# The tail of an attention and mixture kernel takes its PSUM banks in the order of their simulated release

## The chip, the cores and the metric

The kernel runs on one core of a Trainium2 chip. The metric is the device time of one execution in microseconds (us); what counts is the median of several executions. A profiled execution has its own time, and its span (first to last instruction) lies inside that time.

## What is computed

Sliding-window attention with sinks over 4 batches of 8 heads, 768 positions and 64 dimensions, and behind it a soft mixture of 8 experts over the 3072 tokens that come out. The part that this change touches is the mixture's end:

```python
slot_input = (d.T @ x).reshape(E, S_per_e, D)          # 8 experts, 4 slots each, D = 512
for e in range(E):
    h = np.maximum(slot_input[e] @ w1[e], 0.0)         # first layer, F = 1024
    slot_out[e] = h @ w2[e]                            # second layer
return (c @ slot_out.reshape(n_slots, D)).astype(np.float32)   # combine: 3072 x 512
```

All of it is float32. The two weight tensors hold 32 MB, the output 6.29 MB.

## The kernel before

The program has two parts that stand one behind the other on every engine.

The first part is the attention and everything up to `slot_input` (called `si` in the code) and the combine weights. Its steps are written down as entries of a `Plan`, and `Plan.order` simulates them with written-out costs: for each engine a list in `ORDER` fixes which step follows which, and the simulation only interleaves the engines and hands out the eight PSUM banks (512 floats per partition each). `Plan.issue` then emits the instructions. A step that opens a PSUM tile takes a bank that the simulation holds free; the step that reads the tile last gives it back. `banks[b]` is the simulated time at which bank b came free.

The last steps of this part are: `finish` (fin.0 to fin.10), which builds `si` and the factors `rz`; the softmax over slots of the last batch (sm.0 to sm.4); and `turn` (tr.0 to tr.26), nine times two transposes on TensorE with a copy out of PSUM into `ct`, the transposed combine weights. The program's names show `ct` and its sources as `pts` or `qt`, since they lie in those buffers. In VectorE's list of `ORDER` the end reads `..., 922, 926, 966, 927, 929, 963, 930, 969, 925`. In words: the copy of `si` out of PSUM, the softmax's row minimum, a `turn` copy, two softmax steps, a `turn` copy, a softmax step, a `turn` copy, and the reciprocal that ends `finish`.

The second part is `Moe.tail`, emitted in the order in which it is written. It takes its PSUM tiles through `InOrder`, a plan whose `add` runs each step at once. `InOrder` has a fixed rotation: the pair of banks 0 and 1 for the one wide tile (`op`, line 564), and banks 2, 3, 4, 5, 6, 7, 2, ... in turn for all others (`at`, lines 284 to 292). The tail does:

- `first(0, k)` for k = 0 to 3 into two new banks `hp`: 32 matmuls of 512 columns, `si` against weight tiles `wts[0]` to `wts[7]`. Four matmuls on four column groups of the array stand side by side. Each float32 matmul is two rows of the trace.
- `relu(0)`, then `first(1, k)` into two new banks, with `turned(0)` (eight transposes, two banks) behind k = 1, then `relu(1)` and three more `turn` steps.
- `second(r, k, h)`: 96 matmul groups of 256 columns against `wts[16]` to `wts[31]`, into the wide pair `op`.
- `split(h)` and `combine(n, h)`: 24 combine tiles, each copied out of PSUM and sent to the output, 16 transfers of 256 KB and 4 of 512 KB on SyncE's queue.

The weights lie in 21 slots that are used in rotation. Twenty-three weight tiles are loaded by the first part. The last nine are asked for inside the tail by `more(n)`: two behind `first(0, 0)`, two behind `first(0, 1)`, one behind `relu(0)`, and four in the second round. Each goes into a slot that TensorE has to have read first, so these loads wait for the tail's matmuls. All loads and all outputs stand in SyncE's one queue.

Of the kernel before, what the change touches and what calls it, by code (L numbers as in the profile page):

```python
# [125 lines left out]
class Engine:  # L126


    def __init__(self, tc, engine):
        self.tc, self.engine = tc, engine  # L130
# [19 lines left out]
class Plan:  # L150
# [17 lines left out]
    def add(self, key, eng, time, fn, r=(), w=(), new=None, last=None, mode=(128, 128), size=0):  # L168

        self.steps.append((key, eng, time if isinstance(time, tuple) else (time,) * len(eng), fn, tuple(r), tuple(w),  # L170
                           self.some(new), self.some(last), mode if isinstance(mode[0], tuple) else (mode, mode), size))
# [22 lines left out]
    def order(self):  # L194
        steps, self.opened = self.steps, set()
        before = self.depends()
        nxt, left, ready = [[] for _ in steps], [len(d) for d in before], [0.0] * len(steps)
        for i, d in enumerate(before):
            for x in d:
                nxt[x].append(i)  # L200
        closers = {}
        for st in steps:
            for h in st[7]:
                closers[h["name"]] = closers.get(h["name"], 0) + 1
        ends, free, banks = dict.fromkeys(closers, 0.0), dict(self.START), dict.fromkeys(range(8), 0.0)
        todo = {e: list(reversed(o)) for e, o in ORDER.items()}
        on = {i: e for e, o in ORDER.items() for i in o}
        order, mode, place, since = [], (128, 128), 0, 0.0
        while len(order) < len(steps):
            best = None  # L210
            for e, o in todo.items():
                if not o or left[o[-1]]:
                    continue
                i = o[-1]
                t, new = max(free[e], ready[i]), steps[i][6]
                if new:
                    if new[0]["kind"] == "s":
                        x = min((max(banks[y], banks[y + 1]) for y in range(0, 8, 2) if y in banks and y + 1 in banks), default=None)
                    else:
                        x = sorted(banks.values())[len(new) - 1] if len(banks) >= len(new) else None  # L220
                    if x is None:
                        continue
                    t = max(t, x)
                if best is None or t < best[0]:
                    best = (t, e)
            at, e = best
            i, t0 = todo[e].pop(), at
            _, eng, times, _, _, _, new, last, modes, size = steps[i]
            time = times[eng.index(e)]
            if e == "P":  # L230
                t0 += self.SWITCH * (modes[0] != mode)
                mode = modes[1]
            for h in new:
                if h["kind"] == "s":
                    b = max((x for x in range(0, 8, 2) if x in banks and x + 1 in banks
                             and max(banks[x], banks[x + 1]) <= at + 1e-9), key=lambda x: (max(banks[x], banks[x + 1]), -x))
                    h["bank"] = (b, b + 1)
                else:
                    b = max((x for x in banks if banks[x] <= at + 1e-9), key=lambda x: (x ^ 1 not in banks, banks[x], -x))
                    h["bank"] = (b,)  # L240
                for x in h["bank"]:
                    del banks[x]
            end = t0 + time
            place += size
            if place >= self.BLOCK:
                place -= self.BLOCK
                t = end - (end - t0) * place / size
                end += max(0.0, since + self.FETCH - t)
                since = max(t, since + self.FETCH)
            free[e] = end  # L250
            for h in last:
                x = h["name"]
                ends[x], closers[x] = max(ends[x], end + self.LAT), closers[x] - 1
                if closers[x] == 0:
                    for b in h["bank"]:
                        banks[b] = ends[x]
            for x in nxt[i]:
                ready[x] = max(ready[x], end + (0.05 if on[x] == e else self.DMA_LAT if e == "D" else self.LAT))
                left[x] -= 1
            order.append((t0, len(order), i, e))  # L260
        return order

    def issue(self):
# [17 lines left out]

class InOrder(Plan):

    at = 2


    def add(self, key, eng, time, fn, r=(), w=(), new=None, last=None, mode=None, size=0):
        for h in self.some(new):
            if h["kind"] == "s":
                h["tile"] = self.place("s", 0)  # L290
            else:
                h["tile"], self.at = self.place("w", self.at), 2 + (self.at - 1) % 6
        fn(eng[0])

    def tile(self, kind="w"):
# [5 lines left out]
class Moe:  # L301
# [207 lines left out]
        plan.add(keys[0], "P", 0.44, go, r=[("cs", x, y)], w=[h["name"]], new=h)  # L509
        plan.add(keys[1], *(("AV", (0.27, 0.33)) if u % 2 else ("VA", (0.33, 0.27))), out, r=[h["name"]], w=[("ct", b, u)], last=h)  # L510

    def tail(self, slot, wts, more, out):
        nc, c, B, si, pool = self.nc, self.c, self.B, self.si, InOrder(self.pools)
        hp, hs, ht = [], None, None

        def first(r, k):
# [50 lines left out]
        def second(r, k, h):  # L567
            for j in range(4):
                if r == 0 or k < 4:
                    w, o = wts[16 + 8 * r + 4 * (k // 4) + j], 512 * (k % 4) + 256 * h  # L570
                else:
                    w, o = wts[28 + 2 * h + k % 4 // 2], 1024 * (k % 2) + 256 * j
                nc.tensor.matmul(op[32 * j:32 * j + 32, h, 0:256], lhsT=ht[:, k, r, j].rearrange("p q i -> p (q i)"),
                                 rhs=w[:, o:o + 256], start=(r == 0 and k == 0), stop=(r == 1 and k == 7),
                                 skip_group_check=True)

        def split(h):
            hi, x = tw[:, 0, 256 * h:256 * h + 256], op[:, h, 0:256]
            nc.scalar.copy(hi, x)
            nc.vector.scalar_tensor_tensor(tw[:, 1, 256 * h:256 * h + 256], hi.bitcast(F32), c.lo_rows, x,  # L580
                                           op0=ALU.mult, op1=ALU.add)
# [4 lines left out]
        def combine(n, h):  # L586
            if h == 0 and n % 2 == 0:
                obs.append(slot().rearrange("p (n i m) -> p n i m", n=2, i=2))
            cols, yp, ob = slice(256 * h, 256 * h + 256), pool.tile(), obs[n // 2][:, n % 2]
            for i in range(2):  # L590
                nc.tensor.matmul(yp[:, 256 * i:256 * i + 256], lhsT=self.ct[n // 3][:, n % 3, i, :], rhs=tw[:, 1, cols],
                                 start=(i == 0), stop=(i == 1), skip_group_check=True)
            (nc.vector.tensor_copy if (n + h) % 2 else nc.scalar.copy)(
                ob[:, :, cols], yp.rearrange("p (i m) -> p i m", i=2))
            if n < HALF:
                nc.sync.dma_start(ov[:, n, :, cols], ob[:, :, cols])
            elif h:
                nc.sync.dma_start(ov[:, n], ob)
# [12 lines left out]
        for k in range(4):  # L611
            second(1, k, 1)
        for n in range(HALF - 2):
            combine(n, 0)
        for k in range(4, 8):
            second(1, k, 1)
        split(1)
        for n in range(HALF - 2, HALF):
            combine(n, 0)
        for n in range(HALF):  # L620
            combine(n, 1)
        for n in range(HALF, 12):
            combine(n, 0)
# [27 lines left out]


NSLOT = 24
HALF = 8
WARM = 8, 10, 24
PT = 4
KIND = {'kt': 'w', 'q': 'w', 'T': 'w', 'sk': 'w', 'xn': 'w', 'x': 'w'}
ORDER = {"P": [
# [63 lines left out]
def window_path(ctx, tc, c, moe, q, k, v, phi, w1, w2, out):  # L722
# [12 lines left out]
    fr = ctx.enter_context(tc.tile_pool(name="fr", bufs=1))  # L735
    slots = ctx.enter_context(tc.tile_pool(name="slots", bufs=NSLOT - 3))

# [286 lines left out]

    for x in range(WARM[1]):
        h = plan.psum()
        add((f"warm.{x}", 0, 0.0), "P", 0.42, lambda e, h=h: busy(e, h), new=h, last=h)

    for n, (b, j) in enumerate(jobs):
        def t(name, k=None, off=0.0, n=n):  # L1030
            return (name, n, off) if k is None else [(f"{name}.{x}", n, off) for x in range(k)]
# [22 lines left out]
        if j == NJ - 1:  # L1054
# [3 lines left out]
            moe.slot_softmax(plan, t("sm", 5), b, [("lg", b, x) for x in range(NJ)] + last)  # L1058
    for i in range(NSLOT - 7):
        add((f"w.{i}", 0, 0.0), "D", 2.6, lambda e: weight())  # L1060
# [20 lines left out]
def window_rest(tc, moe, plan, weight, weights, wts, slot, out):  # L1081
    plan.issue()

    def more(n):
        for _ in range(n):
            weight()

    weights.load(moe.first[1][:, 0:2048])
    moe.nc = Core(tc, ("tensor",))
    moe.tail(slot, wts, more, out)  # L1090


def general_path(ctx, tc, c, moe, ints, q, k, v, phi, w1, w2, out):
# [126 lines left out]
def fused(ctx, tc, q, k, v, n_sink, window, phi, w1, w2, out):  # L1220
# [24 lines left out]
    t = pools[:, 7]  # L1245
    for _ in range(WARM[0]):
        nc.tensor.matmul(t[:, 0:P], lhsT=c.ident, rhs=c.ident, start=True, stop=True)  # L1247
# [47 lines left out]
```

## Time and profile before

| | |
|---|---|
| three executions | 231.56 us median, 228.77 to 233.5 |
| the profiled execution: time | 226.95 us |
| its span | 225.1 us |
| TensorE busy | 196.9 us (87%), mean granted clock 0.955 |
| VectorE, ScalarE, GpSimd busy | 154.9 us, 149.9 us, 131.2 us |
| transfers | 59.50 MB, mean 264 GB/s |
| first part of the program on TensorE | 0 to 168.7 us |
| tail on TensorE | 171.0 to 210.1 us |

All rows are of the one profiled execution; times run from its span's start. In the views of single instructions PE is TensorE's matmul, PEld its weight load, DVE VectorE, ACT ScalarE and SP SyncE, and a group that touches the work of others gives in square brackets how long the engine stood idle before it and which instruction ended that. Most instructions of both parts carry line 136, a recording helper; they are told apart by tile names. The busy time of PE is modelled, so its end is rough.

### The profile page before, as it was taken

Reading aid. Unit: us, or ns where it says so; the run is one execution under the profiler, and the core shown is the slowest. Engines: PE = TensorE matmul, PEld = TensorE weight load, DVE = VectorE, ACT = ScalarE, POOL = GpSimd, SP = SyncE. Lnnn points to the kernel's source line nnn. Section 1 sums busy time; section 2 is a strip of 40 time slices with the busy share of each in tenths; the row PEclk is TensorE's granted clock in tenths of the full one; section 3 lists DMA queues with packets and bytes.
Section 4 is the critical chain, followed back from the end, with each engine's and each line's share of the span. In section 5 each row is a group of like instructions: output and inputs, shape, how many; then the busy total and the mean of one; then the engine's idle time right before and its main releaser. Section 6 shows DMA issues by size and latency. Waiting matters only on the chain.

```text
span 225.1 us, 9484 instructions
## 1 busy us (share of the span) xinstructions
PE 196.9 (87%) x3730; PEld 138.3 (61%) x3730; DVE 154.9 (69%) x423; ACT 149.9 (67%) x614; POOL 131.2 (58%) x274
## 2 busy tenths in 40 slices
PE   7899897999999999999979999998996999999400
PEld 7766675777676767667867766766651235667300
DVE  4499994698989888988967799897784013007600
ACT  2399888699999989989977989987241113016500
POOL 2248988686879988977777699899440320000000
PEclk9999998899999999999978999999996999999955
DMA  4856989983999799899898999799994899977994
GB/s 113 191 133 138 284 202 256 336 194 75 217 284 300 192 267 323 237 222 292 262 315 191 276 215 338 226 416 335 342 416 167 298 425 379 348 237 240 336 359 197
DMA packets 91623, 59.50 MB, mean 264 GB/s; under 512 B 77236, under 2 KB 85428, under 8 KB 90036
## 3 DMA queue, kind: packets, MB, share of 16 engines
q1 hardware_dynamic: 91572, 58.83, 86.7%
q8 instruction: 31, 0.51, 0.9%
q14 instruction: 20, 0.16, 0.2%
HBM read 52.53 MB, written 6.29 MB: 261 GB/s over the span
## 4 chain that ended last, share of the span: by engine, by line
PE 63%; DVE 10%; ACT 8%; POOL 4%; issue 4%; DMA 3%; SPq 1%; ACTq 0%; DVEq 0%; POOLq 0%
PE ps L136 61%; ACT pts L136 6%; DVE first L136 2%; DVE small L136 2%; DMA wt<-in_v_dram 2%; DVE ps L136 2%; PE ps L1247 2%; POOL pts L136 1%; DMA first<-in_k_dram 1%; POOL small L136 1%; ACT first L136 1%; POOL wt L136 1%; SPq L136 1%; DVE wt L136 1%; ACT qt L136 1%
## 5 line engine op out<-in xcount | busy, mean ns | idle before, releaser
L136 ACT ACTIVATE pts<-ps,small 128x132 f32<-128x132 f32 x192 | 69.0, 390 | 1.2 <-DVE small L136 0.5
L136 PE MATMUL ps<-wt 64*64 64x64 f32 (+4 forms) x1278 | 59.8, 303 | 4.3 <-DMA wt<-in_v_dram 1.1
L136 POOL TENSOR_SCALAR_AFFINE_SELECT wt<-wt 128x512 f32<-128x512 f32 x88 | 53.5, 636 | 4.0 <-DVE wt L136 2.2
L136 PEld LDWEIGHTS ps<-wt 64*64 64x64 f32 (+2 forms) x1278 | 40.2, 130 | 19.5 <-issue 8.8
L136 POOL TENSOR_TENSOR pts<-pts,small 128x528 f32<-128x528 f32 x41 | 43.3, 1073 | 14.9 <-DVE small L136 6.7
L136 PE MATMUL ps<-wt,qt 64*64 64x196 f32 (+2 forms) x780 | 44.8, 324 | 1.7 <-ACT qt L136 0.8
L136 ACT ACTIVATION_READ_ACCUMULATOR pts<-ps,small 128x1 f32 x192 | 43.1, 225 | 0.0
L136 DVE TENSOR_REDUCE small<-ps 128x4 f32<-128x528 f32 x48 | 33.9, 707 | 1.7
L136 PEld LDWEIGHTS ps<-wt,qt 64*64 64x64 f32 x780 | 28.7, 133 | 9.9 <-POOL wt L136 1.5
L136 DVE COPY wt<-ps 128x256 f32<-128x256 f32 (+1 forms) x50 | 25.9, 526 | 8.5 <-PE ps L136 4.5
L136 ACT COPY wt<-ps 128x512 f32<-128x512 f32 (+1 forms) x46 | 23.0, 517 | 9.3 <-PE ps L136 7.9
L136 PE MATMUL ps<-ident,first 64*128 64x64 f32 x576 | 26.9, 237 | 0.6
L136 PEld LDWEIGHTS ps<-ident,first 64*128 64x128 f32 x576 | 22.6, 148 | 6.3 <-issue 2.1
L136 DVE COPY_PREDICATED ps<-later,ps 128x256 f32<-128x256 uint8 x48 | 20.1, 419 | 0.7
L136 DVE COPY first<-ps 128x512 f32<-128x512 f32 x25 | 17.1, 686 | 4.0 <-PE ps L136 3.0
L136 PE MATMUL ps<-ident,pts 64*128 64x64 f32 (+1 forms) x396 | 19.0, 230 | 0.2 <-DVE first L136 0.2
L136 ACT COPY first<-ps 128x512 f32<-128x512 f32 x23 | 13.6, 592 | 8.2 <-PE ps L136 7.4
L136 PEld LDWEIGHTS ps<-ident,pts 64*128 64x128 f32 (+1 forms) x396 | 15.4, 140 | 5.3 <-POOL small L136 3.4
L136 PE MATMUL ps<-wt,si 128*32 128x512 f32 x120 | 15.6, 646 | 2.3 <-DVE pts L136 2.3
L136 POOL TENSOR_TENSOR small<-pts,small 128x32 f32<-128x32 f32 x48 | 12.5, 261 | 3.9
L136 ACT ACTIVATE qt<-ps 128x256 f32<-128x256 f32 x30 | 11.5, 414 | 3.4 <-DVE small L136 2.1
L136 POOL COPY wt<-wt 128x256 f32<-128x256 f32 (+1 forms) x21 | 6.6, 322 | 10.9 <-ACT wt L136 9.1
(129 smaller groups left out, 242.2 us busy)
## 6 DMA issues: line engine op xcount, KB each, us to landing
wt<-in_moe_w_dram SPq DMA_DIRECT2D x26, 1024.0 KB, 6.3
first<-in_k_dram SPq DMA_DIRECT2D x48, 128.0 KB, 3.7
first<-in_q_dram SPq DMA_DIRECT2D x48, 128.0 KB, 4.2
wt<-in_v_dram SPq DMA_DIRECT2D x24, 256.0 KB, 5.2
wt<-in_moe_w_dram SPq DMA_DIRECT2D x8, 512.0 KB, 10.0
out_dram<-wt SPq DMA_DIRECT2D x16, 256.0 KB, 3.2
first<-in_moe_w_dram SPq DMA_DIRECT2D x2, 1024.0 KB
out_dram<-wt SPq DMA_DIRECT2D x4, 512.0 KB, 4.8
```

The costliest lines, as they stand in the source:

```text
L136: return self.tc.keep_in_program_order(f(*args, **kw))
L1247: nc.tensor.matmul(t[:, 0:P], lhsT=c.ident, rhs=c.ident, start=True, stop=True)
```

## The change

`Plan.order` keeps, at its end, the eight banks sorted by the simulated time of their last release (`released`). `InOrder` takes this list. The pair that holds the bank released last becomes the wide tile's, and the six other banks become the rotation, earliest first. `tail` hands the list on. `general_path`, which does not run on these inputs, gets the default order 0 to 7.

```diff
+        self.released = sorted(banks, key=banks.get)
         return order
 
 class InOrder(Plan):
 
-    at = 2
+    def __init__(self, banks, released=range(8)):
 
+        super().__init__(banks)
+        last = released[-1] // 2 * 2
+        self.pair, self.ring = last, [b for b in released if b // 2 * 2 != last]
 
     def add(self, key, eng, time, fn, r=(), w=(), new=None, last=None, mode=None, size=0):
         for h in self.some(new):
             if h["kind"] == "s":
-                h["tile"] = self.place("s", 0)
+                h["tile"] = self.place("s", self.pair)
             else:
-                h["tile"], self.at = self.place("w", self.at), 2 + (self.at - 1) % 6
+                h["tile"] = self.place("w", self.ring[0])
+                self.ring = self.ring[1:] + self.ring[:1]
 
-    def tail(self, slot, wts, more, out):
-        nc, c, B, si, pool = self.nc, self.c, self.B, self.si, InOrder(self.pools)
+    def tail(self, slot, wts, more, out, released=range(8)):
+        nc, c, B, si, pool = self.nc, self.c, self.B, self.si, InOrder(self.pools, released)
 
-    moe.tail(slot, wts, more, out)
+    moe.tail(slot, wts, more, out, plan.released)
```

For this program `released` is 7, 6, 0, 3, 5, 2, 1, 4. In the order of these banks, the steps that free them are a `turn` copy, a step of `finish`, the copy of `si`, a `turn` copy on VectorE, one on ScalarE, two more on VectorE, and the reciprocal `rz`. So the pair is banks 4 and 5, and the rotation 7, 6, 0, 3, 2, 1. The tail's tiles in order of use:

| tile | bank before | bank now |
|---|---|---|
| `hp` of `first(0, k)` | 2, 3 | 7, 6 |
| `hp` of `first(1, k)` | 4, 5 | 0, 3 |
| `turned(0)` | 6, 7 | 2, 1 |
| three `turn` | 2, 3, 4 | 7, 6, 0 |
| `op` (wide) | 0 and 1 | 4 and 5 |
| `turned(1)` | 5, 6 | 3, 2 |
| `combine`, on in rotation | 7, 2, 3, ... | 1, 7, 6, ... |

TensorE's rows at the border of the two parts, before (-) and now (+). `pts` is the last pair of `turn` transposes, `wt,si` are `first(0, k)` and `first(1, 0)`, `first(1, 1)`, and `ident,wt` is `turned(0)`. In brackets stand the engines whose counts an instruction waits for:

```order
 L136 MATMUL ps<-ident,pts 128x128
 L136 MATMUL ps<-wt,si 32x512 [waits DVE_49]
-L136 MATMUL ps<-wt,si 32x512 x31
+L136 MATMUL ps<-wt,si 32x512 x35
 L136 MATMUL ps<-wt,si 32x512 [waits DVE_49]
-L136 MATMUL ps<-wt,si 32x512 x3
-L136 MATMUL ps<-wt,si 32x512 [waits Activation_49]
 L136 MATMUL ps<-wt,si 32x512 x11
 L136 MATMUL ps<-ident,wt 128x128 [waits DVE_49,Activation_49]
```

No matmul moves. The first one waits for VectorE in both programs, but for another count: before for VectorE's instruction 382, now for instruction 375. In the second round (matmul 33) a wait for VectorE's 385 is gone, at matmul 37 a wait for ScalarE has become one for VectorE's 377. VectorE, ScalarE, GpSimd and SyncE have the same rows in the same order in both programs.

VectorE's rows there, the same before and now. The first `si<-ps` is instruction 375, the `pts<-ps` behind the row minimum `rm` is 377, the `pts<-ps` behind the second `RECIPROCAL rs` is 382, and `rz<-ps` is 385:

```order
L136 COPY si<-ps 128x2x2x32
L136 TENSOR_REDUCE rm<-call 128x6
L136 CAST pts<-ps 128x256
L136 TENSOR_TENSOR call<-call,rm 128x192
L136 TENSOR_REDUCE rs<-call 128x6
L136 TENSOR_SCALAR rs<-rs 128x6
L136 RECIPROCAL rs<-rs 128x6
L136 CAST pts<-ps 128x256
L136 TENSOR_TENSOR call<-call,rs 128x192
L136 CAST pts<-ps 128x256
L136 RECIPROCAL rz<-ps 128x1
```

The instruction that the tail's first matmul waits for now stands seven places ahead of the one that it waited for before. The other differences are line numbers and a constant (`WARM`) that stands two lines higher.

## Rows read from the trace of the kernel before

**Rows 1.** The chain that ended last, its end: start us, us, what.

```profile
171.00 34.33 PE ps L136 x418
206.30 3.83 PE ps L136 x28
211.03 0.68 DVE wt L593
```

**Rows 2.** Stretches: length, busy PE, PEld, DVE, ACT, POOL, then PEclk, DMA share, GB/s.

```profile
168.00:169.00 1.00, 0.74 (x6) 0.48 (x5) 1.00 (x4) 0.00 (x0) 0.00 (x0) 1.00 1.04 361
170.00:171.00 1.00, 0.00 (x0) 0.00 (x0) 0.93 (x5) 0.09 (x1) 0.00 (x0) 0.75 1.00 410
171.00:172.00 1.00, 1.00 (x8) 0.34 (x12) 0.62 (x3) 0.00 (x0) 0.00 (x0) 0.50 0.26 107
173.00:174.00 1.00, 1.00 (x8) 0.20 (x4) 0.00 (x0) 0.00 (x0) 0.00 (x0) 0.54 0.00 0
174.00:175.00 1.00, 1.00 (x12) 0.24 (x8) 0.00 (x0) 0.00 (x0) 0.00 (x0) 1.00 0.00 0
175.00:176.00 1.00, 1.00 (x16) 0.35 (x12) 0.00 (x0) 0.00 (x0) 0.00 (x0) 1.00 0.70 139
178.00:182.00 4.00, 4.00 (x44) 1.18 (x40) 0.75 (x1) 0.69 (x1) 3.68 (x7) 1.00 1.01 424
194.00:198.00 4.00, 4.00 (x81) 2.37 (x77) 0.00 (x0) 0.00 (x0) 0.00 (x0) 1.00 1.09 347
218.00:222.00 4.00, 0.00 (x0) 0.00 (x0) 0.00 (x0) 0.00 (x0) 0.00 (x0) 0.50 1.01 400
```

**Rows 3.** Timeline at the border of the two parts: start us, us, instruction [idle before].

```profile
168.23 0.29 DVE L136 COPY si<-ps 128x128 f32<-128x128 f32 x1
168.30 0.44 PE L136 MATMUL ps<-ident,pts 128*128 128x128 f32 x2
...
168.70 0.42 DVE L136 CAST pts<-ps 128x256 fp32r<-128x256 f32 x1
...
169.87 0.35 DVE L136 TENSOR_REDUCE rs<-call 128x6 f32<-128x192 f32 x1 [0.49 <-ACT call L136]
...
170.56 0.38 DVE L136 CAST pts<-ps 128x256 fp32r<-128x256 f32 x1
...
171.00 1.94 PE L136 MATMUL ps<-wt,si 128*32 128x512 f32 x8 [2.26 <-DVE pts L136]
...
171.46 0.15 DVE L136 RECIPROCAL rz<-ps 128x1 f32<-128x1 f32 x1
```

**Rows 4.** Timeline, weight loads of the tail's first matmuls, one row per half pass.

```profile
171.86 0.20 PEld L136 LDWEIGHTS ps<-wt,si 128*32 128x32 f32 x4 [0.66 <-issue]
...
174.17 0.12 PEld L136 LDWEIGHTS ps<-wt,si 128*32 128x32 f32 x4 [0.41 <-issue]
...
174.60 0.12 PEld L136 LDWEIGHTS ps<-wt,si 128*32 128x32 f32 x4 [0.31 <-issue]
```

**Rows 5.** Timeline of PE after an earlier idle gap: start us, us, instruction [idle before].

```profile
115.39 0.27 PE L136 MATMUL ps<-ident,lt 128*128 128x128 f32 x1 [1.38 <-DVE first L136]
```

**Rows 6.** Half-microsecond stretches behind that gap: length, busy PE, PEclk, DMA share, GB/s.

```profile
115.50:116.00 0.50, 0.50 (x13) 0.89 1.13 363
...
119.00:119.50 0.50, 0.50 (x20) 0.70 1.05 224
```

**Rows 7.** Timeline of SyncE's queue in the tail: start us, us, instruction.

```profile
174.38 21.36 SPq L136 DMA_DIRECT2D wt<-in_moe_w_dram  x13
202.94 12.20 SPq L596 DMA_DIRECT2D out_dram<-wt  x16
```

**Rows 8.** Timeline of SyncE's queue, the issue of the load of `wts[27]` alone.

```profile
179.53 0.33 SPq L136 DMA_DIRECT2D wt<-in_moe_w_dram  x1
```

**Rows 9.** Transfers from the weights issued between 179 and 180.5 us: time to landing.

```profile
DMA to landing us min/median/max: 11.6/11.6/11.6
```

**Rows 10.** Timeline of PE, the last matmul of `second(0, 7, 0)` against `wts[22]`.

```profile
192.83 0.38 PE L136 MATMUL ps<-first,wt 128*32 128x256 f32 x1
```

More of the change, by code (lines that the diff above doesn't have):

```diff
@@ L653 @@
 NSLOT = 24
+WARM = 8, 10, 24
 HALF = 8
-WARM = 8, 10, 24
 PT = 4
```

## The prediction

> **What bounds the kernel now.** I read the chain of waits first, from its end [rows 1]. From 171.00 us on it is one piece of TensorE, 34.33 us and 418 instructions long without a wait, then the first combine tiles, then VectorE's last copies at 211 us. The chain does not list the transfers, so the view by stretches comes next [rows 2]. Behind 211 us only the output is left, with the DMA engines at a share of 1.01. The output cannot begin before the tail's first combine, whose first transfer is issued at 202.94 us [rows 7]. So the end hangs on when the tail's matmuls begin and how fast they run: whatever they gain at their start is handed on through `second`, `split` and `combine` to the output.
>
> At that start the timeline shows a hole [rows 3]. TensorE's last `turn` transposes begin at 168.30 and end at 168.74 us. The next matmul, the first of `first(0, 0)`, begins at 171.00 us after 2.26 us of idle time, and the one that let it go is a VectorE copy from PSUM to `pts` that runs from 170.56 to 170.94 us. It is the `turn` copy that gives back bank 2. It has been ready for long, but stands in VectorE's queue behind the softmax of the last batch, which itself waits 0.49 us for ScalarE's exponential (the row at 169.87 us). The data of the matmul, `si`, were in place at 168.23 + 0.29 = 168.52 us. So for 2.26 us nothing is missing but a bank.
>
> Two more things go wrong because of the hole. TensorE's granted clock is 1.00 until after 170 us, averages 0.75 over 170 to 171 us and is 0.50 from there [rows 2], which puts its fall to 1.2 GHz at about 170.5 us; over 173 to 174 us it averages 0.54, which puts the return to 2.4 GHz at 173.9 us. And the DMA engines, at a share of 1.00 over 170 to 171 us, run dry: 0.26, later 0.00, and 0.70 again in 175 to 176 us, so they stand empty from about 171.3 to 175.3 us. The loads inside the tail wait for slots that these matmuls must read first, and the first of the 13 is issued at 174.38 us [rows 7].
>
> **The change, part by part.** The wait first. The tail's first tiles move from banks 2 and 3 to 7 and 6, and the first matmul's wait moves from VectorE's instruction 382 to 375, which is the copy of `si`, done at 168.52 us [rows 3]. TensorE is busy with its own transposes until 168.74 us, so it starts there, with 0.06 us for the handover (from the copy's end at 170.94 to 171.00 us it is as much): 168.8 us. That is 171.0 - 168.8 = **2.2 us**.
>
> The clock second. Twelve groups of four matmuls make up the first 96 rows, and each group is two half passes of four rows. The half passes that start under the low clock begin at 171.00 and 171.86 us and so on, four of them until the one at 174.17 us; from there the spacing is 174.60 - 174.17 = 0.43 us [rows 4]. So four half passes took 174.17 - 171.00 = 3.17 us, and at the high clock take 4 x 0.43 = 1.72 us. That is **1.45 us** more if the clock does not fall. What TensorE does before decides that. In the case with the wait it idles for 2.26 us. There is an earlier place where it idles for 1.38 us, until 115.39 us [rows 5]; there too the clock falls, inside the half microsecond from 115.5 us with its mean of 0.89, and comes back inside the one from 119.0 us [rows 6]. Up to the hole of this change the clock was 1.00, and now TensorE goes on without it. I take the whole 1.45 us; the lower bound is 0, if the clock falls for as long all the same.
>
> The Trainium skill (TensorE: Matmul & The Clock Gate, section HAM oscillation — how this bites in real kernels) warns only of idle gaps on TensorE that are longer than this one. By that rule a gap of 2.26 us costs no clock, and the sum would be 2.2 us alone. The trace speaks against it, since the granted clock falls to 0.50 before the gap ends [rows 2]; I go by the trace and keep the rule as a rival.
>
> The other edits at nothing. The second pair `hp` moves from 4, 5 to 0, 3: the waits it has then are for copies that end at 168.52 and 168.70 + 0.42 = 169.12 us [rows 3], long before `first(1, 0)`. Bank 2, the late one, is now the first tile of `turned(0)`, whose transposes come behind all 96 rows, at 168.8 + 24 x 0.43 = 179.1 us at the earliest, and its copy ends at 170.94 us, 8 us before. Bank 1, the second tile, has its copy right behind that. The wide tile goes to banks 4 and 5; bank 4 is given back by the reciprocal `rz<-ps` at 171.46 + 0.15 = 171.61 us, and `op` is first written behind the second round, so over 7 us later. If these covers were gone, each would cost the distance to its copy, at most the 2.8 us from 168.8 to 171.61. `relu(0)` needs that same `rz`, but comes 16 half passes of 0.43 us behind the start, at 175.7 us, so there are 4 us of cover. In the rotation of six every tile meets the same earlier tiles as before from there on. VectorE, ScalarE, GpSimd and SyncE do the same instructions.
>
> **Where the stall goes, and the transfers.** A gain of 3.65 us on TensorE is only worth that if the weights keep up. `wts[27]` is issued at 179.53 us [rows 8] and lands 11.6 us later, at 191.1 us [rows 9]; it is read first by `second(1, 0, 0)`, right behind the last matmul against `wts[22]` at 192.83 us [rows 10], so by 193.0 us. The margin is 1.9 us. The loads are issued by TensorE's progress, so they move too: the first from 174.38 to 168.8 + 1.72 + 0.21 = 170.7 us, with 0.21 us being 174.38 - 174.17. At that time the DMA engines are still busy with earlier loads, until about 171.3 us, so new data follows almost without a pause, from 170.7 + (175.3 - 174.4) = 171.6 us where it was 175.3 us before. The transfers gain 3.7 us, as much as TensorE, and keep the margin. At 178 us as at 198 us they run at a share above 1.00 [rows 2], so this margin is all that TensorE has. The output then begins 3.6 us earlier and takes as long as before.
>
> **The sum.** 2.2 + 1.45 = 3.65 us, taken as 3.6. Against the profiled execution: 226.95 - 3.6 = 223.3 us (its span 225.1 to 221.5, with 1.85 us around it kept). That execution lies 4.6 us below the median of the three runs, 231.56 us. The hole follows from the order of VectorE's queue and so should be in each of them. On the median's scale the forecast is 231.56 - 3.6 = **228.0 us**, 1.6% less.
>
> **The rivals.**
> - *The gap is not what lowers the clock*, but the light work of the stretch before it (a share of 0.74 in 168 to 169 us, with the small matmuls of `finish`), and the clock falls all the same. Only the wait is gained: 231.56 - 2.2 = 229.4 us. For it: the gap is short. Against: the clock stayed at 1.00 through that work, and another gap, shorter still, was followed by a low clock too [rows 2, 5, 6]. The Trainium skill's rule on gaps, named above, would give this same time.
> - *The weights give part of it back.* If the loads gain less than TensorE does, by more than the 1.9 us of margin, TensorE waits before `second(1, 0, 0)`. Were the loads not to move at all, it would lose 3.65 - 1.9 = 1.75 us: 231.56 - 1.9 = 229.7 us. Against: the DMA engines did stand empty for 4 us [rows 2].
> - *Slower: the loads of the tail get in the way of the loads before them and the stream slows down.* Place: the wait for `wts[27]`. It decides if `wts[27]` lands behind 193.0 us despite being issued 3.6 us earlier. Five tiles came in from 175.3 to 191.1 us, 15.8 us; they would have to take 193.0 - 171.6 = 21.4 us, a third more. Each microsecond beyond is one lost, and a wait of over 1.4 us would bring the low clock with another 1.45 us: with 3 us beyond, 231.56 + 3 + 1.45 = 236.0 us. Against: the same loads in the same order ran at 424 and 347 GB/s with shares above 1.00 [rows 2], and none of the bytes are new.
> - *The change doesn't do what it says*, as the simulated order of release isn't the real one. Then the wait stays: 231.6 us. Against: the trace has the copies that free banks 0, 3, 2 and 4 in the simulated order, and 7 and 6 were freed by instructions of VectorE that stand ahead of the copy of `si` [rows 3].
>
> **How the numbers follow.** The forecast gets 0.75, the clock rival 0.10, the weights 0.07, slower 0.04, no effect 0.04. The range has to cover runs that scatter: the median of new runs may lie as far below 228.0 us as the profiled execution lies below the old median, 223.4 us, and upward it takes in both smaller gains with half of the upper spread (233.5 - 231.56) / 2 = 1 us, so 229.7 + 1 = 230.7, and I go to 231.2 us. The low end is 223.4 us. Two per cent, about what a measurement of this kernel can tell from no change, is 4.6 us; the mechanism alone gives about 4 us at most (the time for which the DMA engines stood empty), so only scatter between medians brings it over: 0.24. Within 2%: 0.71. Slower by over 2%: 0.05.
>
> **What would show it.** Right: in the trace after, the first matmul against `wt,si` begins within 0.2 us of the end of the transposes before it, near 168.8 us; the granted clock is 1.00 from 165 to 210 us; the weight loads of that row group are 0.43 us apart from the first; the DMA share has no stretch at 0 behind 171 us; the first of the 13 loads is issued near 170.7 us and the first output near 199.3 us. Wrong: an idle time before that matmul with VectorE named, or a low clock without one, or a wait of `second` for a weight load.

## The result and the profile after

Five executions of the changed kernel took 222.15 us in the median (221.06 to 227.44), five of the kernel before that stand against them 229.22 us (227.2 to 233.5). The ratio is 0.9705, with a 95% interval of 0.9623 to 0.9787; the ratios in this text leave out the slower executions of either kernel, so they differ a little from those of the medians. The prediction was 228.0 us, 1.6% less than before, with a range of 223.4 to 231.2 us. So the direction was right, the time lies below the range, and the gain of 7.1 us is twice the 3.6 us forecast.

The profiled execution of the changed kernel took 224.88 us, its span is 222.9 us. Its chain of waits, the parts that matter (start us, us, what):

```profile
90.60 2.19 issue
...
169.45 34.05 PE ps L136 x426
...
204.46 3.84 PE ps L136 x28
...
209.20 0.68 DVE wt L598
```

TensorE's long piece now begins at 169.45 us and takes in the last steps of the first part and the tail, where the chain of the kernel before started anew at 171.00 us [rows 1]. The timeline at the border:

```profile
170.15 0.29 DVE L136 COPY si<-ps 128x128 f32<-128x128 f32 x1
170.22 0.20 PEld L136 LDWEIGHTS ps<-ident,pts 128*128 128x128 f32 x2
170.22 0.44 PE L136 MATMUL ps<-ident,pts 128*128 128x128 f32 x2
...
170.59 0.16 PEld L136 LDWEIGHTS ps<-wt,si 128*32 128x32 f32 x8 [0.17 <-DVE si L136]
170.59 2.78 PE L136 MATMUL ps<-wt,si 128*32 128x512 f32 x24
...
171.04 0.13 PEld L136 LDWEIGHTS ps<-wt,si 128*32 128x32 f32 x4 [0.30 <-issue]
...
171.47 0.13 PEld L136 LDWEIGHTS ps<-wt,si 128*32 128x32 f32 x4 [0.30 <-issue]
...
172.48 0.38 DVE L136 CAST pts<-ps 128x256 fp32r<-128x256 f32 x1
...
181.03 1.16 PE L136 MATMUL ps<-ident,wt 128*128 128x128 f32 x8
```

The tail's first matmul follows the transposes without idle time. Its weight load waits 0.17 us for `si` and for nothing else. The copy that it used to wait for runs at 172.48 us, 1.9 us after it, and holds nobody up. From the first half pass on the spacing is 171.47 - 171.04 = 0.43 us, where it was 0.86 us in the first four [rows 4]. The stretches behind it (length, busy PE, PEld, DVE, ACT, POOL, then PEclk, DMA share, GB/s):

```profile
170.00:171.00 1.00, 1.00 (x9) 0.55 (x12) 1.00 (x5) 0.00 (x0) 0.00 (x0) 1.00 1.02 377
173.00:174.00 1.00, 1.00 (x12) 0.26 (x8) 0.54 (x3) 0.00 (x0) 0.00 (x0) 1.00 0.83 197
174.00:175.00 1.00, 1.00 (x16) 0.35 (x12) 0.00 (x0) 0.00 (x0) 0.00 (x0) 1.00 0.80 262
198.00:202.00 4.00, 4.00 (x64) 2.69 (x60) 1.76 (x4) 1.88 (x4) 0.00 (x0) 1.00 0.26 80
```

The clock stays at 1.00, and the DMA share dips to 0.80 where it went to 0.00 before [rows 2]. The transfers do run dry later, between the last weights and the first output: the last row's mean of 0.26 holds a share of 0.00 from 201 to 202 us. The kernel before has the same pause, 0.00 from 203 to 204 us. SyncE's queue (start us, us, instruction) shows the first load of the tail and the first output:

```profile
172.54 21.21 SPq L136 DMA_DIRECT2D wt<-in_moe_w_dram  x13
201.10 12.22 SPq L601 DMA_DIRECT2D out_dram<-wt  x16
```

Counted from the start of the last transposes, the first load comes after 2.3 us (before: 174.38 - 168.30 = 6.1 us [rows 3, 7]), the first output after 30.9 us (before 34.6), and the span ends after 222.9 - 170.22 = 52.7 us (before 225.1 - 168.30 = 56.8). So the tail gains 4.1 us in these two traces. But the spans differ by 2.2 us only: the first part, which has the same instructions in both programs, took 1.9 us longer in this execution. And the medians differ by 7.1 us. The tail alone explains neither number, so the question is what the rest is.

### The profile page after: what moved, and what is told of

Same layout as the page of the kernel before. It is cut to its first block, busy times and chain, and to the rows that moved or that the text cites. A ratio compares the mean times of both kernels' runs of the same rounds, so it can differ in the third digit from the quotient of the medians.

```text
span 222.9 us, 9484 instructions
## 1 busy us (share of the span) xinstructions
PE 194.7 (87%) x3730; PEld 136.9 (61%) x3730; DVE 155.6 (70%) x423; ACT 150.1 (67%) x614; POOL 131.0 (59%) x274
## 4 chain that ended last, share of the span: by engine, by line
PE 62%; DMA 8%; ACT 7%; DVE 6%; issue 4%; POOL 4%; SPq 2%; ACTq 0%; DVEq 0%; POOLq 0%
PE ps L136 61%; DMA first<-in_q_dram 5%; ACT pts L136 4%; DMA first<-in_k_dram 3%; SPq L136 2%; DVE first L136 2%; PE ps L1252 2%; POOL pts L136 1%; POOL small L136 1%; POOL wt L136 1%; ACT first L136 1%; DVE small L136 1%; DVE ps L136 1%; ACT qt L136 1%; ACT wt L136 1%
## 5 line engine op out<-in xcount | busy, mean ns | idle before, releaser
L136 PE MATMUL ps<-wt 64*64 64x64 f32 (+4 forms) x1278 | 58.9, 301 | 3.9 <-ACT pts L136 0.8
L136 PE MATMUL ps<-wt,qt 64*64 64x196 f32 (+2 forms) x780 | 45.6, 328 | 1.4 <-DVE first L136 0.5
L136 ACT ACTIVATION_READ_ACCUMULATOR pts<-ps,small 128x1 f32 x192 | 42.6, 222 | 0.0
L136 PEld LDWEIGHTS ps<-ident,first 64*128 64x128 f32 x576 | 21.5, 139 | 8.6 <-issue 2.2
L136 PE MATMUL ps<-wt,si 128*32 128x512 f32 x120 | 14.1, 594 | 0.0
```

What stands on the lines that cost most here:

```text
L136: return self.tc.keep_in_program_order(f(*args, **kw))
```

## The experiments

Three theories. **A**: the change is worth what it does at the border, 3.6 to 4.1 us, and the rest of the measured 7 us is scatter of the first part. **B**: in other executions the border costs more than in the one I read. **C**: something beyond the border gains about 3 us, as the other bank numbers.

All fourteen traces of this study at a glance, in us from the start of the last transposes of the first part. That start itself, counted from the beginning of the span, is the second column:

| kernel | transposes at | first tail matmul | first output | span end |
|---|---|---|---|---|
| before | 168.30 | 2.70 | 34.64 | 56.8 |
| r_before | 170.77 | 2.70 | 34.91 | 56.6 |
| b_loads | 169.29 | 2.70 | 34.91 | 56.7 |
| after | 170.22 | 0.37 | 30.88 | 52.7 |
| r_after | 172.28 | 0.36 | 30.87 | 52.7 |
| r_after2 | 169.99 | 0.36 | 30.87 | 52.6 |
| a_loads | 171.78 | 0.37 | 30.88 | 53.0 |
| e_six | 169.27 | 0.37 | 30.88 | 52.7 |
| e_queue | 167.57 | 0.61 | 31.12 | 53.0 |
| e_warm | 165.69 | 2.69 | 33.21 | 55.0 |
| e_late | 169.60 | 0.37 | 32.58 | 54.7 |
| e_early | 166.21 | 0.37 | 29.15 | 51.8 |
| best | 168.69 | 0.37 | 29.37 | 52.1 |
| e_shift | 177.67 | 0.37 | 30.88 | 53.0 |

### The two kernels once more

`r_before` is the kernel before with no edit, `r_after` and `r_after2` are the changed kernel with no edit.

> The kernel before once more, against itself: how far two medians of one and the same program lie apart, and what its trace shows in another execution. Theory A (the change is worth the wait and the clock at the border, 3.6 to 4.1 us, and the rest of the measured 7 us is scatter of the first part, which both kernels share): a ratio of 1.00 with an interval of about a per cent, single executions 227 to 233 us, and again a hole of 2.2 to 2.3 us in front of the tail with the low clock behind it. Theory B (in other executions the border costs more than in the one that I read): the hole or the stretch at 1.2 GHz is longer by 2 to 3 us here. Theory C (the other bank numbers make the tail or the whole program faster, about 3 us beyond the border) says nothing of this run.

> The changed kernel once more. Theory A: with more executions the ratio moves toward 0.983 (3.6 to 4.1 us of 230); from the last transposes in front of the tail to the end of the span it takes 52.7 us again where the kernel before takes 56.8. Theory B and theory C: the ratio stays near 0.970 (7 us).

> The changed kernel a third time, for the size of the gain. Theory A (3.9 to 4.1 us at the border, the rest of the first measurement's 7 us was scatter of the first part): ratio 0.982 within 0.006, tail from the last transposes to the span's end 52.7 us. Theory C (something beyond the border, about 3 us): ratio 0.970.

Measured: `r_before` against the kernel before 0.995 (0.988 to 1.002), `r_after` 0.976 (0.971 to 0.981), `r_after2` 0.996 (0.991 to 1.002). Two measurements of one and the same program, each with five rounds, lie two per cent apart and outside of each other's interval. The executions beneath them, all of them counted:

| session | before: executions, mean | changed: executions, mean | difference |
|---|---|---|---|
| first measurement | 5, 230.05 us | 5, 223.46 us | 6.6 us |
| with r_before and r_after | 29, 227.98 us | 6, 224.17 us | 3.8 us |
| with r_after2 | 11, 227.80 us | 6, 225.79 us | 2.0 us |
| together | 45, 228.17 us | 17, 224.53 us | 3.6 us |

The standard deviation of single executions is 1.9 us before and 2.0 us now. By these, the difference of 3.6 us has a 95% interval of 2.5 to 4.8 us, if the sessions are taken as alike. They may not be: 6.6, 3.8 and 2.0 us lie further apart than this scatter would often make them. The first measurement had the highest mean of the kernel before and the lowest of the changed one. Of the border, r_before shows the same picture as [rows 3] (start us, us, instruction):

```profile
170.77 0.44 PE L136 MATMUL ps<-ident,pts 128*128 128x128 f32 x2
173.47 12.20 PE L136 MATMUL ps<-wt,si 128*32 128x512 f32 x96 [2.26 <-DVE pts L136]
185.60 1.16 PE L136 MATMUL ps<-ident,wt 128*128 128x128 f32 x8
```

The hole is 2.26 us again, and the 96 rows take 185.60 - 173.47 = 12.13 us (182.86 - 171.00 = 11.86 in the first trace of before, 181.03 - 170.59 = 10.44 now). The row that ends them in the first trace of before:

```profile
182.86 1.16 PE L136 MATMUL ps<-ident,wt 128*128 128x128 f32 x8
```

Only 0.3 us more than in the first trace, and b_loads has the same border once more: three traces give no sign of theory B. The pooled 3.6 us, and the 3.9 to 4.2 us of the traces, speak against theory C. The next two kernels test it.

### Other ways to the same first bank

`e_six` starts the old rotation at another bank, `e_queue` keeps banks 2 and 3 and moves the copy that frees bank 2 in VectorE's list.

```diff
 e_six:    in tail, of the kernel before
+        pool.at = 6
 e_queue:  in ORDER["V"], of the kernel before
-914, 923, 970, 922, 926, 966, 927, 929, 963, 930, 969, 925
+914, 923, 970, 922, 963, 926, 966, 927, 929, 930, 969, 925
```

> The kernel before with one number changed: the tail's rotation begins at bank 6 and not at bank 2, so the first tiles are 6 and 7, the second 2 and 3, and the wide tile keeps banks 0 and 1. The first matmul then waits for the copy of si, as in the changed kernel. Theory A and theory B: the same time as the changed kernel within 0.5 us, no hole, clock 1.00. Theory C: it falls short of the changed kernel by up to 3 us, since most banks of the tail differ from it.

> The kernel before, banks 2 and 3 first as it has them, with one number moved in VectorE's list: the turn copy that frees bank 2 stands right behind the copy of si, ahead of the softmax, and not six places later. The bank is then free about 0.4 us behind si, at the transposes' end plus 0.2 us. Theory A: the hole shrinks to about 0.25 us, the clock stays at 1.00, and from the last transposes to the span's end it takes 52.9 to 53.0 us, as good as the changed kernel. Theory C (the new bank numbers themselves): it stays near the 56.7 us of the kernel before, but for the hole.

Measured: e_six 222.52 us in the median, ratio 0.969 (0.964 to 0.975); its tail takes 52.7 us, as in the changed kernel, though most of its banks differ. Its six executions have a mean of 222.6 us, 1.6 us below those of r_after beside it, which their scatter can make. e_queue 224.47 us, ratio 0.988 (0.979 to 0.996); its tail takes 53.0 us. The border of e_queue:

```profile
167.57 0.44 PE L136 MATMUL ps<-ident,pts 128*128 128x128 f32 x2
167.71 0.41 DVE L136 CAST pts<-ps 128x256 fp32r<-128x256 f32 x1
...
168.18 2.35 PE L136 MATMUL ps<-wt,si 128*32 128x512 f32 x20 [0.17 <-DVE pts L136]
```

The first matmul waits 0.17 us for the same copy as in the kernel before, and comes 0.24 us later than in the changed one; that is all that the two differ by at the first output (31.12 against 30.88 us). With the old bank numbers and all but 0.2 us of the wait gone, all but 0.3 us of the gain is there. So theory C falls for the tail: the gain there is the wait of the first tile and what follows from it; the rest of the new order changes nothing that these traces show.

### The clock alone

```diff
 e_warm:   in tail, of the kernel before
         hp = [pool.tile() for _ in range(2)]
+        for _ in range(10):
+            nc.tensor.matmul(self.pools[:, 7, 0:P], lhsT=c.ident, rhs=c.ident, start=True, stop=True)
         for k in range(4):
             first(0, k)
```

> The kernel before with ten extra 128x128 matmuls of the identity into bank 7 ahead of the tail's first matmul, about 2.1 us that fit into the hole of 2.26 us. The wait stays, TensorE does not stand idle in it. Theory A: the clock stays at 1.00 and 1.4 us of the 3.65 come back, the first matmul still begins about 2.2 us behind the transposes, and from those to the end of the span it takes about 55.4 us. If the clock falls all the same, nothing comes back (56.8 us).

Measured: 226.21 us in the median, ratio 0.988 (0.982 to 0.993). TensorE in the trace:

```profile
165.69 0.44 PE L136 MATMUL ps<-ident,pts 128*128 128x128 f32 x2
165.96 2.40 PE L136 MATMUL ps<-ident 128*128 128x128 f32 x20
168.38 10.51 PE L136 MATMUL ps<-wt,si 128*32 128x512 f32 x96
178.82 1.16 PE L136 MATMUL ps<-ident,wt 128*128 128x128 f32 x8
```

The first matmul of the tail comes 2.69 us after the transposes, as late as before, but the 96 rows take 178.82 - 168.38 = 10.44 us, as in the changed kernel, with the clock at 1.00. From the transposes to the first output it takes 33.2 us, 1.4 to 1.7 us less than in before, r_before and b_loads. So the low clock comes from the gap and costs 1.4 to 1.7 us, and the rest, 33.2 - 30.9 = 2.3 us, is the wait.

### The loads alone

```diff
 e_late:   in tail, of the changed kernel (more(1, t) loads into the tile t)
             first(0, k)
-            if k < 2:
-                more(2)
+            if k == 2:
+                t, bank = slot(), self.pools[:, 2, 0:2]
+                nc.tensor.matmul(bank, lhsT=c.ident, rhs=c.ident[:, 0:2], start=True, stop=True)
+                nc.scalar.copy(t[:, 0:2], bank)
+                more(1, t)
+                more(3)
```

> The changed kernel with the first of the tail's loads held back: it also waits for two columns that ScalarE writes into its slot behind first(0, 2), so the 13 loads begin about 3.7 us later, nearly as late as in the kernel before, while TensorE begins at once. Theory A with the margin of the prediction (1.9 to 2.0 us at wts[27]): TensorE waits about 1.7 us in front of second(1, 0, 0) with a transfer named, and the tail takes 54.4 us in place of 52.7. If the transfers had no part in it, 52.7 us; if they were what bounds the tail, 56.4 us.

Measured: 226.59 us, ratio 0.997 (0.989 to 1.004). The loads begin 175.86 - 169.97 = 5.9 us behind the first matmul, where it is 172.54 - 170.59 = 1.95 us in the changed kernel, so 3.9 us later. The first output comes 1.7 us later and the end 2.0 us later (54.7 against 52.7). TensorE, the queue, and the chain of waits with the load that released it:

```profile
192.30 3.44 PE L136 MATMUL ps<-wt 128*32 128x256 f32 x59 [0.67 <-DMA wt<-in_moe_w_dram]
```

```profile
175.86 20.94 SPq L136 DMA_DIRECT2D wt<-in_moe_w_dram  x13
```

```profile
178.17 14.00 DMA wt<-in_moe_w_dram
```

TensorE waits for weights. It stands idle for 0.67 us and not for the 1.7 expected, in part because the added matmul holds it up ahead of that place: the 96 rows with it take 10.88 us in place of 10.44. The load decides when it goes on. A delay of 3.9 us cost 1.7 us at the first output and 2.0 at the end, so the margin was 1.9 to 2.2 us, where the prediction had 1.9. Without the loads' share of the change about half of its gain would be given back: that half of the earlier start is worth something only because the loads start earlier too.

### A further step, and the scatter

```diff
 e_early:  in tail, of the changed kernel
-        for k in range(8):
+        for k in range(4):
             second(0, k, 1)
 ...
         for n in range(HALF - 2):
             combine(n, 0)
+        for k in range(4, 8):
+            second(0, k, 1)
         for k in range(4, 8):
             second(1, k, 1)
```

> A further step on the changed kernel: four of the eight second(0, k, 1) move from ahead of split(0) to behind the first six combine tiles, so the output begins earlier, into the stretch in which the transfers run dry between the last weights and the first output. The weights of split(0), wts[28] and wts[29], land about 2.2 us ahead of their use in the changed kernel, and four steps are 1.7 us. Expected: the first output 1.7 us earlier, 51.0 us from the last transposes to the span's end if the output bounds the rest; 52.7 us if TensorE's last tiles do.

Measured: 224.46 us, ratio 0.977 (0.967 to 0.986). The first output comes 30.88 - 29.15 = 1.73 us earlier, as expected, but the end only 0.9 us earlier. The output runs dry once more, while TensorE works through what was moved (columns as above):

```profile
201.00:202.00 1.00, 1.00 (x11) 1.00 (x10) 1.00 (x2) 0.78 (x2) 0.00 (x0) 1.00 0.53 174
```

The tail explains about 4 of the 7.1 us. For the rest I read the first part. Its length, the second column of the table, goes from 165.7 to 172.3 us among kernels whose first part has the same instructions (all but b_loads, a_loads, best and e_shift; in e_queue one copy near its end stands earlier), while the tail of one program repeats to 0.2 us. The `acc` update, one per token step, marks the way. From the fourth to the fifth it is 14.5 us in one group of traces and 18.7 to 20.1 us in another (VectorE's timeline of e_six, then of the changed kernel):

```profile
83.34 0.48 DVE L136 SCALAR_TENSOR_TENSOR acc<-acc,sums,ps 128x257 f32<-128x257 f32 x1
```

```profile
97.83 0.47 DVE L136 SCALAR_TENSOR_TENSOR acc<-acc,sums,ps 128x257 f32<-128x257 f32 x1
```

```profile
81.92 0.48 DVE L136 SCALAR_TENSOR_TENSOR acc<-acc,sums,ps 128x257 f32<-128x257 f32 x1
```

```profile
100.92 0.47 DVE L136 SCALAR_TENSOR_TENSOR acc<-acc,sums,ps 128x257 f32<-128x257 f32 x1
```

Of the ten traces with that same first part, r_before, after, r_after, r_after2 and e_late are in the long group, and before, e_six, e_warm, e_queue and e_early in the short one. In each of the long ones TensorE stops inside the same group of 16 transposes, after the ninth. The changed kernel, with the granted clock behind it, and r_after:

```profile
90.13 0.47 PE L136 MATMUL ps<-ident,pts 64*128 64x64 f32 x9
92.79 0.41 PE L136 MATMUL ps<-ident,pts 64*128 64x64 f32 x7 [2.19 <-issue]
```

```profile
93.00:94.00 1.00, 1.00 (x28) 0.95 1.26 293
94.00:95.00 1.00, 1.00 (x20) 0.50 0.55 123
```

```profile
94.84 0.40 PE L136 MATMUL ps<-ident,pts 64*128 64x64 f32 x7 [2.47 <-issue]
```

TensorE waits 2.2 to 2.7 us for nothing that these views name, then runs at the low clock, as behind the gap at the border. Between the two updates it costs 4.2 to 5.6 us; at the end of the first part the long traces are 3.2 us behind the short ones on average (170.6 against 167.4 us). All three traces of the changed kernel have it, so the change does not remove it. Over the 58 executions of before in the later sessions the mean clock goes with the time: the 17 with a mean clock of 0.951 or less took 229.5 us on average, the seven with 0.970 or more 225.8 us.

Two kernels moved two weight loads that SyncE issues shortly ahead of the stop, a third one joined this with e_early, a fourth moved TensorE's instructions.

```diff
 b_loads (of before), a_loads (of the changed kernel), best (of e_early): in ORDER["D"]
-542, 544, 947, 939, 615, ... 697, 936, 632, ... 945, 943, 857
+542, 544, 615, ... 697, 936, 947, 632, ... 945, 943, 939, 857
 best: besides, all eight combine(n, 0) stand ahead of the late second(0, k, 1)
 e_shift (of the changed kernel): behind the eight warm-up matmuls
+    for _ in range(16):
+        nc.tensor.matmul(t[:, 0:2], lhsT=c.ident, rhs=c.ident[:, 0:2], start=True, stop=True)
```

> The kernel before with two 1 MB weight loads of the first part moved later in SyncE's list (947 and 939, asked for near 84 us, now behind 936 and behind 943). Five of ten traces so far have TensorE standing for 2.2 to 2.7 us with nothing waited for in the middle of one and the same group of 16 transposes near 90 us, and the low clock behind it, 4.4 us in all, in kernels of either kind. Theory A in its present form (that stop is what spreads the runs): without the two loads the stop is gone, the spread of single executions falls from 1.7 us (standard deviation) to about 1 us and the mean from 228.0 to about 225.8 us; the hole in front of the tail stays at 2.26 us. If the two loads have no part in it, the stop is there in half the traces and nothing changes.

> The changed kernel with the same two loads moved. Against the run before this one, in which the first part is the same and should be steady, it gives the size of the change without the scatter. Theory A: 4.0 us less than that run (3.65 by the prediction, 4.1 by the traces), so a mean of about 221.8 us. Theory C: 7 us less.

> The changed kernel, the two loads moved, and the tail's order of e_early with all eight first combine tiles ahead of the four late second(0, k, 1), since in e_early the output ran dry once more between the sixth tile and split(1). Expected: 51.2 us from the last transposes to the span's end (51.8 in e_early), about 1.5 us less than the run before this one, near 220.3 us.

> The changed kernel with sixteen tiny matmuls of two columns more at its very start, which move every later TensorE instruction 32 matmul rows and as many weight loads further back. If the stop near 90 us belongs to a place in the instruction stream, it comes 32 rows earlier among the work, so inside the value matmuls ahead of those 16 transposes, or not at all in this one look (it was there in half the traces). If it belongs to the work, it splits the same transposes 9 to 7 again.

Measured: the stop near 90 us is absent from all three traces with the loads moved (14.5 to 15.4 us between the two updates). But the mean of b_loads is 230.6 us, more than the 229.1 us of before beside it (ratio 1.010, 0.998 to 1.022), and its spread 3.1 us; I had expected 225.8 and 1. The moved loads hold up others, and TensorE now waits for the values near 146 and 157 us (b_loads):

```profile
146.26 1.53 PE L136 MATMUL ps<-wt 64*64 64x64 f32 x36 [1.60 <-DMA wt<-in_v_dram]
...
157.18 1.53 PE L136 MATMUL ps<-wt 64*64 64x64 f32 x36 [1.60 <-DMA wt<-in_v_dram]
```

So, as far as six executions tell, the scatter was not removed, and these two kernels are no steady pair: a_loads, mean 226.5 us, lies 4.0 us below b_loads, as theory A had it, but with six executions each that alone would prove little. In best the mean is 225.0 us over twelve executions, 4.1 us below before beside it (ratio 0.988, 0.983 to 0.994), and its tail takes 52.1 us where 51.2 was expected; it is no better than e_early.

In e_shift, of which there is one execution of 232.45 us, the fourth and the fifth update are 15.4 us apart and there is no stop in those transposes. TensorE stops three times without a named cause, for 1.31 us until 37.44 us, for 0.69 us until 98.83 us and for 0.63 us until 123.18 us. The first two:

```profile
37.44 0.56 PE L136 MATMUL ps<-wt,qt 64*64 64x196 f32 x7 [1.31 <-issue]
...
98.83 0.88 PE L136 MATMUL ps<-wt 64*64 64x192 f32 x20 [0.69 <-issue]
```

The second is the one that this run was made to find. It stands inside the value matmuls ahead of the 16 transposes, 31 rows earlier among the work, and has 1732 matmul rows of TensorE ahead of it where the stop of the five long traces has 1731. It is shorter, and the clock stays at 1.00 behind it. That speaks for a place in the instruction stream rather than in the work, though it is one trace.

What is at that place can be read from the transfers that the traces keep. The page of every run lists 31 transfers of kind `instruction`, of 16 KB each, on queue q8; e_shift has 32, with more instructions on TensorE alone, so by this count they bring TensorE's instructions. In the five long traces the thirteenth begins 7.6 to 8.4 us behind the twelfth, within 0.4 us of the moment at which TensorE stops, and TensorE goes on 1.3 to 1.5 us after it has come in (in the changed kernel it takes from 90.49 to 91.46 us, and the next row begins at 92.79). In e_shift it is 7.6 us behind the twelfth, and TensorE goes on 1.4 us after its end. In the eight traces without the stop it begins 4.2 to 5.6 us behind the twelfth. So TensorE seems to stand there for want of its own instructions. No run set this time on purpose, and why the transfer comes late in some executions stays open. The first part of this trace was also longer than in any other, 177.7 us, for reasons that stay open.

## Why the prediction was right or wrong

**The wait: right.** It named the bank, the copy on VectorE and the 2.2 us. Measured, the first matmul moves from 2.70 to 0.37 us behind the transposes, 2.33 us; the 0.13 us more lie in the modelled end of the transposes, since the next matmul begins before it. Banks 0, 3, 2, 1, 4 and 5 cost nothing, as it said.

**The clock: right.** 1.45 us was forecast, 1.42 (before) and 1.69 us (r_before, b_loads) measured by the 96 rows, and e_warm shows it by itself. The rival in which the clock falls all the same is out. The Trainium skill (TensorE: Matmul & The Clock Gate, section HAM oscillation — how this bites in real kernels) warns only of longer gaps; the traces do not agree, since behind 2.26 us the clock was at 0.50 in before, r_before and b_loads, and the measurement decides.

**The transfers: right, but for one sign.** First load 1.95 us behind the first matmul (forecast 170.7 - 168.8 = 1.9), margin 1.9 to 2.2 us by e_late, no wait of `second` for a load in any trace of the changed kernel. The rivals on the weights are out, the slower one included. The sign that failed is "the DMA share has no stretch at 0 behind 171 us": it is 0.00 from 201 to 202 us, where the weights are in and the output has not begun, and the kernel before had that pause too. It changes nothing in the sum.

**The sum: slightly short.** 3.65 us forecast for the tail; the first output comes 34.64 - 30.88 = 3.76 us earlier against the trace it was made from, 4.0 against the other two, and the span end 3.9 to 4.2 us. The pooled executions give 3.6 us; that this meets the forecast to the tenth is luck, since its interval is 2.5 to 4.8 us.

**The scale and the range: wrong.** The step that failed is "On the median's scale the forecast is 231.56 - 3.6". Three executions stood behind 231.56 us. The mean of 63 executions of that program in this study is 228.4 us, with single ones from 224.4 to 233.5; the same sum from there gives 224.8 us, and the 17 executions of the changed kernel have a mean of 224.5. Of the 5.85 us between the forecast of 228.0 and the measured 222.15 us, 3.2 are this scale. The other 2.7 are five executions of the changed kernel whose median lies below what the sum gives from 228.4; by the 17 together that is scatter. The profiled execution lay 4.6 us below the median of the three, which the prediction noted and explained by nothing; it was a sign that the time outside the tail scatters by several us. The range was then built from the spread of these few numbers and from rivals of the border, and had no term for the first part. The chance of 0.24 for faster by over 2% rested on scatter, and was too small for a spread of 2 us in single executions.

**What stays open** is why the transfer of instructions near 90 us comes late in some executions, and whether the first measurement's 6.6 us in means were chance alone. The pooled executions and the repeatable tail speak for it; they do not prove it for those ten, of which one was traced.

## What to carry to other kernels

Where one part of a program hands PSUM banks to the next, look which instruction gives back the bank that is taken first and what stands ahead of it in its queue; moving either the bank or the copy brought nearly the same here (tails of 52.7 and 53.0 us). Price a gap on TensorE with what follows it: here 2.3 us of waiting also cost 1.4 to 1.7 us of clock, and let the DMA engines run dry for 4 us. When executions scatter by more than the change is worth, compare the stage in the traces (here from one instruction to the span's end, the same to 0.2 us between traces of one program) and take the scale from many executions, or give a ratio and no time.

## What the runs showed of the hardware that was not expected

TensorE stopped for 2.2 to 2.7 us in the middle of a group of equal transposes, with the profile naming no wait, at the same instruction in five of ten traces. The clock then went to 0.50 for about 3 us (in the changed kernel from about 94 to 97 us), and the step took 4.2 to 5.6 us longer. In all five, and in e_shift, a 16 KB transfer of instructions came in 1.3 to 1.5 us before TensorE went on. Ratios with intervals of 0.5 to 0.8 per cent to each side came out at 0.971, 0.976 and 0.996 for one and the same pair of programs, so such an interval does not hold what changes from one session to the next.
